# A convolution stem's gradients on one core: the weight gradient's tiles of two batches laid side by side, and the order of all engines planned with other transfer costs

## The chip, the core and the metric

The kernel runs on one core of a Trainium2 chip. The metric is device microseconds of one launch on that core; a figure for a kernel is the median of several runs. A profile is one execution of its own, recorded by the hardware profiler.

The core has engines that run side by side: TensorE (PE; its weight loads are PEld), VectorE (DVE), ScalarE (ACT), GpSimd (POOL) and SyncE (SP), which issues nearly all transfers here. All of them take their instructions in order, each from a queue of its own, and wait for each other by semaphores. A transfer runs on 16 DMA engines after it has been issued.

## What is computed

A strided convolution over time, a normalisation over the whole sequence, GELU, and then all gradients. B = 2 batches, T = 16000 steps, D = 256 channels, K = 31 taps, stride 2, L = 7985 outputs, all in bf16:

```python
h = jnp.einsum('blc,cd->bld', x[:, 0:s * L:s, :], w[0])
for i in range(1, K):
    h = h + jnp.einsum('blc,cd->bld', x[:, i:i + s * L:s, :], w[i])
mu = jnp.einsum('bld->bd', h)[:, None, :] / L
var = jnp.einsum('bld->bd', (h - mu) ** 2)[:, None, :] / L
h = (h - mu) / jnp.sqrt(var + 1e-5)
h = h * gn_gamma[None, None, :] + gn_beta[None, None, :]
return _gelu(h)
```

The outputs are this result and, for a given `grad_out`, the gradients of x, of w (31 x 256 x 256), of gamma and of beta.

## The kernel before, in words

**Stages.** F0 is the forward convolution of batch 0; F1 that of batch 1, with normalisation and GELU of batch 0 beside it; G0 is the gradient of x for batch 0, with GELU of batch 1 beside it; G1 the gradient of x for batch 1; W the gradient of w for both batches. Beside G0 and G1, `dl_turn` turns each piece of the gradient round with DMA transposes (L555) and writes it to DRAM (`dld`) in 128 KB pieces (L550), from where W reads it.

**The arithmetic.** The convolution is split by the bits of the tap number into nested fast convolutions: at each of three levels a pair of taps gives three products, A (the first), C (the second) and B (of the sums), in place of four. In W the two outer levels make nine parts (`COMBOS`, a loop `n` over 0 to 8), the third level is done inside a part. So a part needs sums of x tiles and differences of gradient tiles, made by DVE: `w_add` (L1533) adds two x tiles of 128 x 4096, `pair_x` (L1630) adds neighbouring columns of x tiles, `leaf_d` (L1713) and `pair_d` (L1639) subtract rows of the gradient tiles. The matmuls of W (`w_mm`, L1565) take these sums as they are done; `w_emit` (L1594) adds up finished taps and sends them out.

**Tiles of W.** All of SBUF is one tile, `arena`; the kernel hands out byte ranges of it by hand (`sb(offset, shape)`). For each part and batch there are two x tiles (`x_tile`, loaded by `x_raw`, 1 MB each, in 1 KB runs) and one gradient tile `D2` of 19 rows of 256 columns (`d_tile`): ten even rows and nine odd ones, in two transfers of 640 and 576 KB. Two sets of x tiles, `XS_` and `XT_`, serve even and odd parts; the next part's are loaded while this one computes.

**One instruction for both batches.** `both(u, v, dims)` (L1623) makes an access pattern whose outermost step is the distance from batch 0's view to batch 1's. `pair_x`, `pair_d` and `leaf_d` use it for their inputs and outputs, so that one DVE instruction serves both batches, wherever the two tiles lie. In `XS_` the two first tiles lie at bytes 165376 and 190336, and two tiles of `XT_` at 173696 and 182016, between them; the two others of `XS_` lie at 86016 and 40960, so that the step is negative. In `D2_` the tiles of the batches follow each other, so that the step goes over the rest of batch 0's rows.

**The order.** The kernel body records operations with `plan.add(engine, duration, outputs, inputs, function, ...)`. `Plan.cells` (L266) turns the views into 32-byte cells, and operations that share cells depend on each other: it looks at a pattern's real pieces. `Plan.order` (L317) goes backward and gives each operation a due time from TensorE's own order, less a lead: `self.lead` (L53) holds one number per kind of operation and stage, `self.fine` (L162) a further one per part of a stage. `Plan.listing` (L335) then runs a model of the engines and of the DMA queue, with the costs that each `add` was given, and writes at each moment the ready operation with the earliest due time. `emit` builds the instructions in that order, which is held on every engine. The semaphores and their waits are set by the framework afterwards, from the access patterns.

**Costs of transfers.** `load` (L542) charges SP 0.25 + 0.0005 n us for issuing n packets, `turn` (L552, a DMA transpose) 0.15 + 0.00105 n and at least 1.24.

The lines by which the profile names the work: L550 `load`, L555 `turn`, L744 matmuls of F, L1332 matmuls of G, L839 ACT's copies out of PSUM, L1399 sums on DVE in G, L1214 to L1225 `e_comp` (a gradient tile put together), L1234 its spreading by ACT, L1285 differences in G, L690 sums of weights.

Of the kernel before, what the change touches and what calls it, by code (L numbers as in the profile page):

```python
# [12 lines left out]
ACT = mybir.ActivationFunctionType  # L13
ALU = mybir.AluOpType
# [24 lines left out]
class Plan:  # L39
# [3 lines left out]
    def __init__(self, tc):  # L43
# [10 lines left out]
            "F0 f_evac last": -9.0,  # L54
            "F0 f_mm f_leaf": -119.5,
            "F0 f_mm f_outer": -14.0,
            "F0 f_mm f_three_ac": -8.0,
            "F0 f_mm f_three_b": 32.5,
            "F0 f_mm pe_turn": -75.5,
            "F0 f_outer forward": -106.0,  # L60
            "F0 f_seed forward": -12.0,
            "F0 f_three_b forward": -26.5,
            "F0 keep f_evac": -48.0,
            "F0 load f_evac": 33.0,
            "F0 load put": 9.5,
            "F0 load x_load": 13.5,
            "F0 tt f_sums": -72.0,
            "F0 tt third": 4.5,
            "F0 turn w2_part": -15.5,
            "F0 turn x_load": 24.0,  # L70
            "F0 ve f_first": -78.0,
            "F0 ve_neg f_seed": 20.5,
            "F0 w_sub f_first": 12.0,
            "F0 w_sum w2_part": 26.0,
            "F0 zero f_evac": -11.0,
            "F1 f_evac last": -30.0,
            "F1 f_mm f_leaf": -44.0,
            "F1 f_mm f_outer": -28.0,
            "F1 f_mm f_three_ac": 0.5,
            "F1 f_mm f_three_b": -5.5,  # L80
            "F1 f_outer forward": -3.0,
            "F1 f_seed forward": 11.5,
            "F1 f_three_b forward": 4.0,
            "F1 gelu_unit gelu_batch": -1.0,
            "F1 keep f_evac": 15.5,
            "F1 load gelu_unit": 30.0,
            "F1 tiny elem_finalize": -71.5,
            "F1 tt f_sums": -53.0,
            "F1 tt gelu_unit": -16.5,
            "F1 tt second": -25.5,  # L90
            "F1 tt third": -8.0,
            "F1 turn gelu_unit": -8.0,
            "F1 turn x_load": 45.0,
            "F1 ve f_seed": -22.5,
            "F1 ve_neg f_seed": 5.5,
            "F1 zero f_evac": 10.0,
            "G0 cp e_comp": 11.5,
            "G0 g_mm g_three_b": -9.0,
            "G0 g_three_b input_grad": 6.5,
            "G0 gelu_batch conv_stem_kernel": -7.5,  # L100
            "G0 gelu_unit gelu_batch": -1.0,
            "G0 keep g_evac": -7.0,
            "G0 keep g_seed": 6.0,
            "G0 load dl_turn": 8.0,
            "G0 load e_load": 14.5,
            "G0 load g_evac": -13.5,
            "G0 load gelu_unit": 1.5,
            "G0 load load_w2": 19.5,
            "G0 plus g_seed": 5.0,
            "G0 tiny elem_finalize": -9.0,  # L110
            "G0 tt first": -44.0,
            "G0 tt gelu_unit": -0.5,
            "G0 tt second": 1.0,
            "G0 tt third": -10.5,
            "G0 turn gelu_batch": 4.0,
            "G0 w_sum load_w2": -31.0,
            "G0 zero e_comp": 8.0,
            "G0 zero gelu_batch": -63.0,
            "G1 cp e_comp": -17.5,
            "G1 e_comp e_load": 13.0,  # L120
            "G1 g_mm g_leaf": -6.0,
            "G1 g_mm g_outer": -7.0,
            "G1 g_mm g_three_ac": -8.0,
            "G1 g_mm g_three_b": -5.5,
            "G1 g_three_b input_grad": -238.0,
            "G1 keep g_evac": 3.5,
            "G1 load dl_turn": 11.0,
            "G1 load e_load": -5.5,
# [3 lines left out]
            "G1 spread g_seed": -73.5,  # L132
            "G1 tt first": 3.5,
            "G1 tt second": -15.5,
            "G1 tt third": -43.5,
            "G1 turn dl_turn": 3.5,
            "G1 zero e_comp": 0.5,
            "W keep w_keep": -8.0,
            "W keep weight_grad": 1.0,
            "W leaf_d weight_grad": 6.5,  # L140
            "W load d_tile": -32.5,
            "W load out0_late": 21.0,
# [5 lines left out]
            "W turn out0_late": -36.5,  # L148
            "W ve w_done": 31.5,
# [5 lines left out]
            "W w_emit weight_grad": -64.5,  # L155
            "W w_mm w_leaf": 0.5,
            "W w_pairs weight_grad": -65.0,
# [5 lines left out]
            "F0 f_evac last": {1: 13.5, 2: 6.5, 3: -9.0},  # L163
            "F0 f_mm f_outer": {0: 25.5, 2: -12.0, 3: -48.0},
            "F0 f_mm f_three_ac": {0: -9.5, 1: -3.0, 2: -20.5, 3: -3.0},
            "F0 f_mm f_three_b": {0: 3.0, 2: -87.0, 3: -60.5},
            "F0 f_seed forward": {0: 19.5, 2: 58.0},
            "F0 f_three_b forward": {1: 27.0},
            "F0 keep f_evac": {2: 9.5},
            "F0 load f_evac": {0: 47.5, 3: 4.5},  # L170
            "F0 load put": {0: 20.5, 1: -24.0, 2: 28.0},
# [4 lines left out]
            "F0 turn x_load": {0: -17.0, 2: -24.5},  # L176
            "F0 ve f_first": {0: 33.5},
            "F0 ve f_seed": {0: 30.0, 2: 31.5},
            "F0 ve_neg f_seed": {0: 19.5, 2: -68.5, 3: 41.0},
            "F0 w_sum w2_part": {1: 17.0, 2: -9.5, 3: -32.5},  # L180
            "F0 zero f_evac": {3: 28.0},
            "F0 zero x_load": {3: 58.5},
            "F1 f_evac last": {0: 1.5, 1: 15.0},
            "F1 f_mm f_leaf": {2: -59.5, 3: -91.0},
            "F1 f_mm f_three_ac": {1: -39.0, 2: -69.5, 3: -2.5},
            "F1 f_mm f_three_b": {1: 14.5, 2: 2.0},
            "F1 f_outer forward": {3: 2.0},
            "F1 f_seed forward": {3: 3.0},
            "F1 f_three_b forward": {1: 6.5, 3: -28.5},
            "F1 gelu_unit gelu_batch": {0: -28.0, 1: -2.5, 2: 1.0, 4: 0.5, 6: 6.0, 7: 3.0},  # L190
            "F1 keep f_evac": {3: -7.5},
            "F1 load gelu_unit": {0: -17.0, 2: -9.5, 4: 31.0, 5: -40.5},
            "F1 load out0_store": {7: 37.0},
            "F1 tt f_sums": {0: 2.0},
            "F1 tt gelu_unit": {0: 3.5, 6: -46.0},
            "F1 tt third": {1: 27.5, 3: -11.5},
            "F1 turn gelu_batch": {0: -35.5},
            "F1 turn gelu_unit": {0: 58.0, 6: 25.0},
            "F1 turn x_load": {1: 21.0, 2: 15.0, 3: -71.5},
            "F1 ve f_seed": {3: 24.5},  # L200
            "F1 ve_neg f_seed": {3: 2.0},
            "F1 zero f_evac": {3: 5.5},
            "G0 cp e_comp": {0: -9.5, 2: -7.0},
            "G0 e_comp e_load": {0: -19.0, 1: 5.5, 2: -5.0, 3: 19.5},
            "G0 g_mm g_leaf": {0: -1.5, 3: -25.0},
            "G0 g_mm g_three_ac": {0: 0.5, 1: -1.0, 3: 17.5},
# [264 lines left out]
def conv_stem_kernel(  # L471
# [13 lines left out]
    nc = tc.nc  # L485
# [1035 lines left out]
    for k, o in (("early", 110720), ("late", 57344)):  # L1521
        PD[k] = [(sb(o + 4096 * i, 4, 512), sb(o + 8192 + 4096 * i, 2, 4, D)) for i in range(2)]
# [347 lines left out]
```

## Time and profile before

| | before |
|---|---|
| median of 3 runs | 1212.95 us (1208.56 to 1215.85) |
| the profiled execution | 1214.13 us, of which its span is 1212.4 us |
| TensorE busy | 1138.9 us (94%) |
| DVE busy | 982.9 us (81%) |
| ACT busy | 569.1 us (47%) |
| transfers | 243.55 MB, mean 201 GB/s |
| mean granted TensorE clock | 0.980 |

The span goes from the first to the last instruction of the profiled execution. A busy share says how long an engine had an instruction in it; the rest is time in which it waited, and the profile names what ended each wait. A timeline row has the start, the time, the engine, the line, the operation with its output and input, the count, and in brackets the idle time ahead of it with what ended it. In rows of the chain of waits stand start, length and what the time was spent on; for a DMA that is the time from its issue to its landing. The granted clock is the share of the full TensorE clock that the chip allowed in a stretch. By the program, F0 and F1 end around 435 us, G0 and G1 around 865 us, and W fills the rest.

### The profile page before, as it was taken

The numbers are of one execution on the slowest core, as the hardware profiler recorded it, in microseconds if no ns is written. First come the engines' busy times: TensorE is split into PE (matmuls) and PEld (weight loads), VectorE is DVE, ScalarE is ACT, GpSimd is POOL, SyncE is SP. The second block draws the span as 40 slices with busy tenths as digits, with TensorE's granted clock in tenths as the row PEclk, the third lists the DMA queues.
The fourth block names the chain that finished last, engine by engine and source line by source line (L and its number), as shares of the span: only waits on it lengthen the run. The fifth ranks groups of instructions, "written<-read, shape, count | busy, mean of one in ns | idle before, by whom it ended". The sixth has DMA issues, their size and how long they took to land.

```text
span 1212.4 us, 18743 instructions
## 1 busy us (share of the span) xinstructions
PE 1138.9 (94%) x7645; PEld 757.9 (63%) x7700; DVE 982.9 (81%) x856; ACT 569.1 (47%) x849; POOL 27.2 (2%) x77
## 2 busy tenths in 40 slices
PE   5999999999999999899987999999599999898998
PEld 4888899777778944444443434444278666565685
DVE  7988787798999979796866576875599997677995
ACT  1354445688766687886734556544222212111200
POOL 0000000000000110000000000100000000000000
PEclk8999999999999999999999999999899999998999
DMA  9566945889785979998888566676958825988655
GB/s 208 85 145 137 205 129 142 197 184 211 163 187 146 342 241 242 263 235 234 224 192 217 135 178 180 180 187 168 334 145 254 279 95 175 336 262 287 211 153 149
DMA packets 378061, 243.55 MB, mean 201 GB/s; under 512 B 233377, under 2 KB 353831, under 8 KB 373799
## 3 DMA queue, kind: packets, MB, share of 16 engines
q1 hardware_dynamic: 377783, 242.35, 74.4%
q8 instruction: 60, 0.98, 0.3%
q14 instruction: 26, 0.21, 0.1%
q0 software_dynamic: 192, 0.00, 0.0%
HBM read 106.24 MB, written 80.25 MB: 154 GB/s over the span
## 4 chain that ended last, share of the span: by engine, by line
PE 31%; DMA 8%; DVE 7%; SPq 3%; issue 1%; ACT 1%; DVEq 0%; POOL 0%
PE ps L1565 17%; PE ps L1332 13%; DMA arena<-in_x_dram 3%; DMA arena<-dld 3%; DVE arena L1533 2%; SPq L550 2%; DVE ps L1399 1%; DVE arena L1630 1%; DMA arena<-arena 1%; SPq L555 1%; DVE arena L1639 1%; ACT arena L839 1%; DMA dld<-arena 1%; DMA arena<-hd 1%; DVE arena L1713 1%
## 5 line engine op out<-in xcount | busy, mean ns | idle before, releaser
L1332 PE MATMUL ps<-arena 128*128 128x512 bf16 (+1 forms) x1880 | 416.3, 379 | 28.5 <-DVE ps L1399 7.2
L744 PE MATMUL ps<-arena 128*128 128x256 bf16 (+4 forms) x3460 | 408.4, 282 | 12.9 <-DMA arena<-in_x_dram 5.8
L744 PEld LDWEIGHTS <-arena 128*128 128x128 bf16 x3460 | 339.2, 99 | 82.2 <-DMA arena<-in_x_dram 6.1
L1332 PEld LDWEIGHTS <-arena 128*128 128x128 bf16 x1920 | 189.0, 98 | 254.5 <-issue 39.9
L1565 PE MATMUL ps<-arena 128*128 128x256 bf16 (+1 forms) x2305 | 314.8, 299 | 28.4 <-DVE arena L1630 24.9
L1565 PEld LDWEIGHTS <-arena 128*128 128x128 bf16 x2320 | 229.7, 99 | 113.8 <-DVE arena L1630 27.3
L839 ACT ACTIVATE arena<-ps 128x1024 f32<-128x1024 f32 (+1 forms) x143 | 145.3, 1021 | 291.9 <-PE ps L1565 95.7
L702 DVE TENSOR_TENSOR arena<-arena 128x2080 bf16<-128x2080 bf16 (+7 forms) x126 | 156.2, 1264 | 32.3 <-PE ps L744 26.2
L1399 DVE TENSOR_TENSOR ps<-ps,arena 128x2048 f32<-128x2048 f32 x40 | 91.7, 2294 | 20.4 <-PE ps L1332 12.4
L1285 DVE TENSOR_TENSOR arena<-arena 128x1032 bf16<-128x1032 bf16 (+1 forms) x120 | 84.4, 726 | 28.6 <-PE ps L1332 23.2
L1119 DVE TENSOR_TENSOR arena<-arena 128x2048 bf16<-128x2048 bf16 (+1 forms) x80 | 95.5, 1195 | 14.7 <-ACT arena L1111 7.2
L1533 DVE TENSOR_TENSOR arena<-arena 128x4096 bf16<-128x4096 bf16 x38 | 86.2, 2284 | 19.4 <-DMA arena<-in_x_dram 17.9
L1655 ACT COPY ps<-ps 128x256 f32<-128x256 f32 x54 | 19.3, 357 | 93.3 <-PE ps L1565 92.2
L859 ACT ACTIVATE arena<-ps 128x512 bf16<-128x512 f32 (+1 forms) x64 | 37.1, 580 | 52.9 <-PE ps L744 50.3
L1639 DVE TENSOR_TENSOR arena<-arena 128x2048 bf16<-128x2048 bf16 x38 | 46.3, 1221 | 13.5 <-DMA arena<-dld 9.0
L1630 DVE TENSOR_TENSOR arena<-arena 128x4096 bf16<-128x4096 bf16 x19 | 43.3, 2284 | 10.8 <-DMA arena<-in_x_dram 10.4
L1399 DVE TENSOR_TENSOR arena<-ps,arena 128x2048 f32<-128x2048 f32 x16 | 36.6, 2289 | 18.0 <-ACT arena L839 14.6
L1109 DVE SCALAR_TENSOR_TENSOR arena<-arena 128x2048 bf16<-128x2048 bf16 (+1 forms) x16 | 35.8, 2236 | 17.0 <-ACT arena L1106 16.5
L780 ACT ACTIVATE ps<-ps 128x256 f32<-128x256 f32 x75 | 27.8, 371 | 40.0 <-PE ps L744 38.7
L1713 DVE TENSOR_TENSOR arena<-arena 128x4608 bf16<-128x4608 bf16 x18 | 45.6, 2550 | 0.1
L1234 ACT COPY arena<-arena 128x768 bf16<-128x768 bf16 (+1 forms) x64 | 36.5, 616 | 19.2 <-DVE arena L1225 15.8
L814 ACT ACTIVATE arena<-ps 128x512 f32<-128x512 f32 x56 | 29.5, 601 | 25.1 <-PE ps L744 19.7
(78 smaller groups left out, 637.9 us busy)
## 6 DMA issues: line engine op xcount, KB each, us to landing
arena<-in_x_dram SPq DMA_DIRECT2D x40, 1024.0 KB
dld<-arena SPq DMA_DIRECT2D x144, 128.0 KB
arena<-hd SPq DMA_DIRECT2D x32, 512.0 KB
out_dram<-arena SPq DMA_DIRECT2D x14, 1024.0 KB
arena<-dld SPq DMA_DIRECT2D x18, 640.0 KB
arena<-dld SPq DMA_DIRECT2D x18, 576.0 KB
vl<-arena SPq DMA_DIRECT2D x36, 256.0 KB
arena<-vl SPq DMA_DIRECT2D x9, 1024.0 KB
```

What stands on the lines that cost most here:

```text
L702: lambda: nc.vector.tensor_tensor(out=o, in0=a, in1=b, op=ALU.add))
L744: yield nc.tensor.matmul(ps[:, dh, cs], lhsT=wt, rhs=mv, start=s0, stop=False, skip_group_check=True)
L839: lambda: nc.scalar.activation(out=out, in_=ps, func=ACT.Copy, scale=scale))
L1119: add("DVE", dve(nf), [o], [a, b_], lambda: V.tensor_tensor(out=o, in0=a, in1=b_, op=op))
L1285: lambda: nc.vector.tensor_tensor(out=o, in0=a, in1=b, op=ALU.subtract))
L1332: yield nc.tensor.matmul(ps[:, e, 0:wide], lhsT=lt, rhs=mv, start=s0, stop=False, skip_group_check=True)
L1399: lambda: nc.vector.tensor_tensor(out=o, in0=a, in1=b, op=ALU.add))
L1533: add("DVE", dve(4096), [o], [a, b], lambda: nc.vector.tensor_tensor(out=o, in0=a, in1=b, op=ALU.add))
L1565: yield nc.tensor.matmul(ps[:, s, c0:c1], lhsT=lt, rhs=mv, start=s0, stop=False, skip_group_check=True)
L1630: add("DVE", dve(4096), [o], i, lambda: nc.vector.tensor_tensor(out=o.rearrange("p b (f c) -> p b f c", c=512), in0=i[0], in1=i[1], op=ALU ...
L1639: add("DVE", dve(2048), [o], [u, v], lambda o=o, u=u, v=v: nc.vector.tensor_tensor(out=o, in0=u, in1=v, op=ALU.subtract))
L1713: add("DVE", dve(4608), [o], [u, v], lambda: nc.vector.tensor_tensor(out=o, in0=u, in1=v, op=ALU.subtract))
```

## The change

Four things are changed.

1. The gradient tiles of W are laid out anew: the even rows of both batches next to each other (`D2E_`), then the odd rows of both (`D2O_`). The outputs of `pair_d` are interleaved in the same way (`PD`): both batches of one half, then both of the other.
2. `pair_x` takes one instruction for both batches only where the second x tile lies at most 4352 elements behind the first; otherwise it takes two, one per batch. That is so for the five `pair_x` that read `XS_` directly. W has then 179 DVE operations in place of 174.
3. `load` and `turn` charge SP other costs.
4. The two tables of leads are replaced throughout, for all five stages.

The diff, with the tables cut to their first lines:

```diff
@@ Plan.__init__
         self.lead = {
-            "F0 f_evac last": -9.0,
-            "F0 f_mm f_leaf": -119.5,
-            "F0 f_mm f_outer": -14.0,
+            "F0 f_evac last": -14.5,
+            "F0 f_mm f_leaf": -67.5,
+            "F0 f_mm f_outer": 14.0,
...
         self.fine = {
-            "F0 f_evac last": {1: 13.5, 2: 6.5, 3: -9.0},
+            "F0 f_evac last": {0: 17.5, 3: -12.5},
...
@@ load, turn
-        add(eng, {"POOL": 0.74, "SP": 0.25 + 0.0005 * np_, "ACT": 0.4}[eng], [out], [in_],
+        add(eng, {"POOL": 0.74, "SP": 0.42 + 0.00016 * np_, "ACT": 0.4}[eng], [out], [in_],
...
-        add("SP", max(1.24, 0.15 + 0.00105 * np_), [out], [in_],
+        add("SP", max(1.3, 0.15 + 0.00125 * np_), [out], [in_],
...
@@ tiles of W
-    D2_ = [[sb(o + 9728 * i, 19, D) for i in range(2)] for o in (0, 127424)]
+    D2E_ = [[sb(o + 5120 * i, 10, D) for i in range(2)] for o in (0, 127424)]
+    D2O_ = [[sb(o + 10240 + 4608 * i, 9, D) for i in range(2)] for o in (0, 127424)]
...
-    PD = {"all": [(sb(16384 + 4096 * i, 4, 512), sb(o, 2, 4, D)) for i, o in enumerate((73728, 77824))]}
-    for k, o in (("early", 110720), ("late", 57344)):
-        PD[k] = [(sb(o + 4096 * i, 4, 512), sb(o + 8192 + 4096 * i, 2, 4, D)) for i in range(2)]
+    PD = {k: [(sb(o + 4096 * i, 4, 512), sb(u, 2, 2, 4, D)[:, :, i]) for i in range(2)]
+          for k, o, u in (("all", 16384, 73728), ("early", 110720, 118912), ("late", 57344, 65536))}
@@ d_tile
-        for j, (r, k) in enumerate(((0, 10), (10, 9))):
+        for j, (v, k) in enumerate(((D2E_[n > 0][b], 10), (D2O_[n > 0][b], 9))):
             t = dl_d[b][3 * i1 + i2][j]
-            load(D2_[n > 0][b][:, r:r + k].rearrange("p r d -> p (r d)"),
+            load(v.rearrange("p r d -> p (r d)"),
@@ pair_x
-        o = both(p[0][0], p[1][0], [[1, 2048]])
-        i = [both(x[0][:, j], x[1][:, j], [[1024, 4], [1, 512]]) for j in range(2)]
-        add("DVE", dve(4096), [o], i, lambda: nc.vector.tensor_tensor(out=o.rearrange("p b (f c) -> p b f c", c=512),
-                                                                      in0=i[0], in1=i[1], op=ALU.add))
+        if 0 <= x[1].offset - x[0].offset <= 4352:
+            o = both(p[0][0], p[1][0], [[1, 2048]])
+            i = [both(x[0][:, j], x[1][:, j], [[1024, 4], [1, 512]]) for j in range(2)]
+            add("DVE", dve(4096), [o], i, lambda: nc.vector.tensor_tensor(out=o.rearrange("p b (f c) -> p b f c", c=512),
+                                                                          in0=i[0], in1=i[1], op=ALU.add))
+            return
+        for (o, _), v in zip(p, (x[0], x[1])):
+            add("DVE", dve(2048), [o], [v], lambda o=o, v=v: nc.vector.tensor_tensor(
+                out=o, in0=v[:, 0:8:2], in1=v[:, 1:8:2], op=ALU.add))
@@ weight_grad
-            D2, XSUM = D2_[n > 0], XSUM_[n > 0]
+            D2, DO, XSUM = D2E_[n > 0], D2O_[n > 0], XSUM_[n > 0]
...
-                u, v = (both(D2[0][:, k], D2[1][:, k], [[D, 9], [1, D]]) for k in (o_, 10))
+                u, v = (both(t[0][:, k], t[1][:, k], [[D, 9], [1, D]]) for t, k in ((D2, o_), (DO, 0)))
...
-                w_pairs(X[h], h, pm, D2, 11, 2)
-            pair_d(pm, D2, 12, 10, 11)
+                w_pairs(X[h], h, pm, DO, 1, 2)
+            pair_d(pm, DO, 2, 0, 1)
```

More of the change, by code (lines that the diff above doesn't have):

```diff
@@ L81, in __init__ @@
[L81 to L93, printed above, removed]
@@ new lines, in __init__ @@
+            "F0 load f_evac": 62.5,
+            "F0 load put": 10.5,
+            "F0 tt f_sums": -97.0,
+            "F0 tt second": 16.5,
+            "F0 ve_neg f_seed": -25.0,
+            "F0 w_sub f_first": 8.0,
+            "F0 w_sum w2_part": 5.0,
+            "F0 zero x_load": 16.5,
+            "F1 f_evac last": -54.0,
+            "F1 f_mm f_leaf": -235.5,
+            "F1 f_mm f_three_ac": -3.5,
+            "F1 f_mm f_three_b": -20.5,
+            "F1 f_outer forward": 3.5,
+            "F1 f_seed forward": 3.0,
@@ L162, in __init__ @@
         self.fine = {
-            "F0 f_evac last": {1: 13.5, 2: 6.5, 3: -9.0},
[L164 to L171, printed above, removed]
[4 rows of a table removed]
@@ L186, in __init__ @@
[L186 to L195, printed above, removed]
```

291 lines of the change are left out of this document (159 added, 132 removed), and 4 rows, old and new, of the table MIR.

## The prediction

> **What bounds the kernel now.** I read the page first, then busy time by stretch, then who waited for whom on TensorE, then the timelines of the engines around each long gap of TensorE.
>
> ```profile
> span 1212.4 us, 18743 instructions
> ...
> PE 1138.9 (94%) x7645; PEld 757.9 (63%) x7700; DVE 982.9 (81%) x856; ACT 569.1 (47%) x849; POOL 27.2 (2%) x77
> ```
>
> TensorE is busy for 1138.9 of 1212.4 us. The change leaves its 7,700 matmuls as they are, so it can win only what lies between them: 73.5 us, and the time that a halved clock adds to busy time. The table by stretch says where that is (length, then busy time and count of PE, PEld, DVE, ACT, POOL, then granted clock, DMA share, GB/s):
>
> ```profile
> 23.00:435.00 412.00, 411.06 (x3450) 338.47 (x3453) 359.17 (x359) 245.21 (x450) 8.87 (x19) 0.99 0.73 179
> 435.00:634.00 199.00, 186.31 (x848) 84.88 (x863) 164.72 (x177) 148.69 (x172) 9.40 (x23) 0.99 0.88 225
> 634.00:665.00 31.00, 22.54 (x99) 10.03 (x100) 20.67 (x23) 12.17 (x18) 0.58 (x3) 0.94 0.83 216
> 665.00:865.50 200.50, 193.31 (x876) 87.64 (x892) 139.00 (x108) 104.22 (x116) 5.47 (x17) 0.99 0.69 182
> 865.50:881.30 15.80, 0.02 (x1) 0.02 (x2) 6.86 (x4) 1.02 (x1) 0.00 (x0) 0.57 1.10 358
> 881.30:884.80 3.50, 3.50 (x17) 2.52 (x18) 3.50 (x2) 0.00 (x0) 0.00 (x0) 0.51 0.38 86
> ...
> 1056.60:1059.80 3.20, 0.03 (x2) 0.01 (x1) 3.20 (x3) 1.02 (x1) 0.00 (x0) 0.84 1.10 350
> 1059.80:1065.60 5.80, 5.80 (x28) 4.12 (x29) 5.80 (x3) 1.07 (x3) 0.00 (x0) 0.50 1.10 349
> ...
> 1100.90:1106.40 5.50, 0.01 (x2) 0.01 (x1) 5.50 (x4) 1.02 (x1) 0.00 (x0) 0.71 0.84 266
> 1106.40:1110.00 3.60, 3.60 (x18) 2.56 (x19) 3.60 (x3) 1.02 (x1) 0.00 (x0) 0.50 0.89 251
> ```
>
> The forward pass after 23 us has 0.9 us of idle TensorE in 412: nothing to win. The middle (435 to 865.5) idles 12.7 + 8.5 + 7.2 = 28.4 us in many pieces. The weight gradient starts at 865.5 with a hole of 15.8 us and has two more of 3.2 and 5.5 us; behind each of the three TensorE runs at half clock for 3.4, 5.8 and 3.6 us, half of which is lost (1.7, 2.9, 1.8). In all three holes the engine that comes last is DVE with a sum at L1630, `pair_x`.
>
> **The change part by part: the hole at the start of W.** DVE's timeline there, SP's issues, the chain of waits, and the sizes of the transfers:
>
> ```profile
> 861.72 2.28 DVE L1533 TENSOR_TENSOR arena<-arena 128x4096 bf16<-128x4096 bf16 x1
> 874.41 2.29 DVE L1630 TENSOR_TENSOR arena<-arena 128x4096 bf16<-128x4096 bf16 x1 [10.41 <-DMA arena<-in_x_dram]
> ```
> ```profile
> 855.32 1.41 SPq L550 DMA_DIRECT2D arena<-dld  x1
> 858.80 0.55 SPq L550 DMA_DIRECT2D arena<-in_x_dram  x1
> 859.39 2.22 SPq L550 DMA_DIRECT2D arena<-dld  x3
> ```
> ```profile
> 862.15 12.14 DMA arena<-in_x_dram
> ```
> ```profile
> arena<-in_x_dram SPq DMA_DIRECT2D x40, 1024.0 KB
> ...
> arena<-dld SPq DMA_DIRECT2D x18, 640.0 KB
> arena<-dld SPq DMA_DIRECT2D x18, 576.0 KB
> ```
>
> The `pair_x` at 874.41 waits 10.41 us for the transfer issued at 862.15, which lands at 862.15 + 12.14 = 874.29. By the addresses it needs nothing of it: the sum reads the tiles at bytes 165376 and 190336 with one pattern, and the transfer writes the next part's tile at 173696, which lies between them. The build puts a wait on everything that a pattern spans. The change gives this sum its own two instructions, and in the order of the built program with its waits each of the two waits for its own tile alone. Over the whole stage, DVE's waits for a transfer on which no address depends fall from 16 to 2.
>
> What is late next is the last tile that the first matmuls truly need: the transfer issued at 858.80, then a `w_add` (2.28 us) and the other `pair_x` (2.29). I put its landing back from 874.29 by what was issued after it, three `arena<-dld` of 640, 576 and 576 KB and the 1,024 KB of 862.15: 2,816 KB or 2.88 MB, at the 358 GB/s of the stretch 865.5 to 881.3, is 8.1 us, so 866.2. The new order issues both 576 KB halves ahead of it where one 640 KB half was: 512 KB or 1.5 us more, 867.7. The two sums take 4.6, so TensorE starts at 872.3 in place of 881.3: **9.0 us** won. Ends: a load takes from 6.1 us (a row below) to 12.14, so it lands between 864.9 and 870.9, which gives 11.8 to 5.8. The remaining hole of 7 us still ends in a cold start, so the 1.7 us stay lost.
>
> **The holes at 1056 and 1101.** DVE again, and the chain ahead of the second:
>
> ```profile
> 1050.34 4.62 DVE L1533 TENSOR_TENSOR arena<-arena 128x4096 bf16<-128x4096 bf16 x2 [3.69 <-DMA arena<-in_x_dram]
> 1056.31 1.22 DVE L1639 TENSOR_TENSOR arena<-arena 128x2048 bf16<-128x2048 bf16 x1 [1.36 <-DMA arena<-dld]
> 1057.46 2.28 DVE L1630 TENSOR_TENSOR arena<-arena 128x4096 bf16<-128x4096 bf16 x1
> ```
> ```profile
> 1092.14 1.21 DVE L1639 TENSOR_TENSOR arena<-arena 128x2048 bf16<-128x2048 bf16 x1
> 1099.58 1.23 DVE L1639 TENSOR_TENSOR arena<-arena 128x2048 bf16<-128x2048 bf16 x1 [6.23 <-DMA arena<-dld]
> 1100.72 2.28 DVE L1533 TENSOR_TENSOR arena<-arena 128x4096 bf16<-128x4096 bf16 x1
> 1102.92 1.22 DVE L1594 TENSOR_TENSOR arena<-ps,arena 128x1024 bf16<-128x1024 f32 x1
> 1104.06 2.28 DVE L1630 TENSOR_TENSOR arena<-arena 128x4096 bf16<-128x4096 bf16 x1
> ```
> ```profile
> 1079.56 9.21 DMA arena<-in_x_dram
> ...
> 1093.38 6.11 DMA arena<-dld
> ```
>
> At 1056 a `pair_d` (L1639) stands ahead of the `pair_x` and waits for a half of the gradient tile that its pattern spans and does not read. Afterwards only the odd halves are spanned, they are issued first, and in the built order the `pair_x` stands right behind the `w_add`s, which end at 1050.34 + 4.62 = 1054.96: `pair_x` ends at 1057.2, TensorE starts at 1057.3 in place of 1059.8. **2.5 us**, and with a hole of only 0.7 us the clock stays up: **2.9 us** more.
>
> At 1093 the wait is a loop: the transfer of 1093.38 was held back until the `pair_d` of 1092.14 had read, by a span again, and the next `pair_d` then waited 6.23 us for that transfer. Both go. DVE's work behind the last true landing (1079.56 + 9.21 = 1088.77) is in the new order two `w_add`s, a half `pair_x`, the `pair_x` and two `w_emit`s: 2.3 + 2.3 + 1.2 + 2.3 + 2.4 = 10.5, to 1099.3, ahead of the 1100.9 at which TensorE runs out. **5.5 us** and the 1.8 of the cold start. Each of these two terms is nothing at worst, if the tile itself comes later by that much.
>
> **The clock.** For the hole of 3.17 us the price of 2.9 rests on rows; another hole of about that length cost none:
>
> ```profile
> 654.86:657.87 3.01, 0.00 (x1) 0.00 (x0) 2.98 (x4) 0.00 (x0) 0.00 (x0) 1.00 1.05 339
> 657.87:663.00 5.13, 5.08 (x25) 2.54 (x26) 5.13 (x5) 1.02 (x1) 0.00 (x0) 1.00 0.13 18
> ```
>
> So a remainder of some 3 us may or may not keep the loss. The Trainium skill, TensorE: Matmul & The Clock Gate, section on HAM oscillation, asks for no TensorE gaps above about 3.4 us; by it the hole of 3.2 us should have been free, and the row at clock 0.50 behind it says otherwise. By that rule the sum would be better by 2.9 us only if a hole of 3 us remained at 1056; with 0.7 us both give the same.
>
> **The splits.**
>
> ```profile
> L1639 DVE TENSOR_TENSOR arena<-arena 128x2048 bf16<-128x2048 bf16 x38 | 46.3, 1221 | 13.5 <-DMA arena<-dld 9.0 <-PE ps L1565 3.7
> L1630 DVE TENSOR_TENSOR arena<-arena 128x4096 bf16<-128x4096 bf16 x19 | 43.3, 2284 | 10.8 <-DMA arena<-in_x_dram 10.4 <-PE ps L1565 0.2
> ```
>
> Five `pair_x` become two halves each: 2 x 1221 - 2284 = 158 ns, 0.8 us over the stage, hidden beside TensorE except the one at the start, where it is in the wait for the tile. The new strides of the gradient tiles cost nothing that a row shows: sizes and inner runs are the same.
>
> **The order with the measured issue cost.** The planner charged a 128 KB `dld<-arena` 0.25 + 0.0005 x 256 = 0.378 us of SP; it will charge 0.42 + 0.00016 x 256 = 0.461. The rows of SP's issues from 586 to 850, then TensorE, ACT and DVE in that stretch:
>
> ```profile
> L550 SPq DMA_DIRECT2D dld<-arena x100: 367/488/2031, 585.8 to 845.1; - x100
> ```
> ```profile
> 639.46 15.40 PE L1332 MATMUL ps<-arena 128*128 128x512 bf16 x63 [5.34 <-ACT ps L839]
> 657.87 2.32 PE L1332 MATMUL ps<-arena 128*128 128x256 bf16 x11 [3.01 <-DVE ps L1399]
> ```
> ```profile
> 637.66 0.83 ACT L1234 COPY arena<-arena 128x768 bf16<-128x768 bf16 x1 [5.94 <-DVE arena L1225]
> ```
> ```profile
> 630.66 0.81 DVE L1214 TENSOR_SCALAR arena<-arena,stats 128x2048 bf16<-128x2048 bf16 x1 [5.82 <-DMA arena<-hd]
> ```
>
> 100 of these at 0.488 - 0.378 = 0.11 us make 11 us by which SP falls behind the plan in the input gradient. The rows show the effect: DVE waits 5.82 us for an `arena<-hd`, the copy at L1234 behind it on ACT waits 5.94, and ACT's copy out of PSUM that TensorE needs stands in order behind that. The stalls of 5.34 and 3.01 us are 8.4 together. Planned with the true cost, the same transfers are to stand earlier. But all stages are reordered (of SP's 711 issues some 170 leave their place relative to the rest, of DVE's 824 some 190), and the trace cannot show what new stalls come. Upper end: all 28.4 us of the middle; lower end: as many stalls of this kind again, 8 us lost. I take **6 us** won, near the two stalls. The forward pass is reordered too; at 0.9 us of idle it can only lose, 0 to 4; I take 0, since DVE there is busy 359 of 412 and has a tenth to spare.
>
> **The sum**, from the profiled execution's 1214.1 (span 1212.4 and 1.7 around it; 1.2 above the median of the three runs): 9.0 + 2.5 + 2.9 + 5.5 + 1.8 + 6 = 27.7; 1214.1 - 27.7 = 1186.4, say **1187**.
>
> **Rivals.**
>
> *The transfers bound W anyway.* From 1056.6 to 1065.6 the DMA share is 1.10, the highest of the table, and parts that fetch eight 1 MB tiles need them within some 40 us. Then the holes at 1056 and 1101 only change their name, the reorder gives nothing, and 9 us are won: 1205. Against it: at 1065.6 to 1100.9 the share falls to 0.84 while DVE waits on its loop. Its price is a delay of the last tile by 2.5 to 5.5 us at each hole.
>
> *Slower: ACT's in-order queue in the input gradient.* If the new order again puts L1234's copies ahead of the copies out of PSUM while their tile is late, each chunk costs a stall like the 5.34 us one. W wins 21.7 (9.0 + 5.4 + 7.3); it is used up by four such stalls, and with six it is 1214.1 - 21.7 + 32 = 1224. It decides from the fifth chunk on. For it: the chain above exists. Against: it did so at one of the chunks now.
>
> *The patterns still span others.* Then only the reorder is left: 1214.1 - 6 = 1208. The waits in the built order speak against it.
>
> **How the numbers follow.** My forecast and what lies near it (1172 to 1200): 0.79. Transfers bound W: 0.11 (1200 to 1207). Patterns still span: 0.03. Slower by ACT's queue or by another stall of the reorder: 0.07, of which 0.04 by over 0.5%. About 0.5%, 6 us, is what a measurement of this kernel tells from no change. Faster: 0.79 + 0.08 of the rivals = 0.87; within: 0.09; slower: 0.04. Range: the terms' lower ends (11.8, 5.4, 7.3 and 17 of the middle) give 1172; the upper side takes in the transfer rival, 1205.
>
> **What would show it.** In the profile after: the first L1565 matmul of W behind a hole of 5 to 9 us, with an L1630-like half sum no longer waiting for a transfer issued after its own; no hole above 2 us with clock 0.50 in the later parts; DVE's waits `<-DMA arena<-dld` near zero at `pair_d`; idle TensorE between 435 and 865 down from 28 to about 22. I am wrong if `w_add` (L1533) takes over the waits for `in_x_dram` by as much as L1630 and L1639 lose, or if the middle shows more and longer stalls behind ACT.

## The result, and the profile after

| | before | after |
|---|---|---|
| median of four runs (lowest to highest) | 1213.37 us (1208.56 to 1215.85) | 1193.49 us (1190.87 to 1197.82) |
| ratio, 95% interval | | 0.9844 [0.9802, 0.9887] |
| profiled execution / its span | 1214.13 / 1212.4 | 1190.87 / 1189.1 |
| TensorE's last matmul of the input gradient ends | 865.47 | 865.56 |
| hole at the start of W | 15.81 | 5.46 |
| TensorE idle, 435 us to that point | 28.3 | 26.5 |
| TensorE idle in W behind the first hole | 12.6 | 4.4 |

The changed kernel takes 1.56% [1.13, 1.98] less, by this ratio 18.9 us (the medians lie 19.9 apart). (The idle times and the ends are summed from the matmuls' rows of each trace.) The line numbers are some six higher: `w_add` is L1539, `pair_x` L1637 and in halves L1641, `pair_d` L1650, W's matmuls L1571. First the page after, then busy time by stretch (length; PE, PEld, DVE, ACT, POOL; granted clock, DMA share, GB/s), cut at the same stages as the table of before:

```profile
span 1189.1 us, 18747 instructions
...
PE 1136.3 (96%) x7645; PEld 756.0 (64%) x7700; DVE 981.3 (83%) x861; ACT 568.9 (48%) x849; POOL 26.2 (2%) x77
```
```profile
435.00:634.00 199.00, 185.69 (x838) 84.08 (x853) 162.28 (x174) 149.08 (x172) 7.22 (x23) 0.98 0.89 221
634.00:665.00 31.00, 25.04 (x108) 10.95 (x108) 18.36 (x21) 10.81 (x16) 0.58 (x3) 0.94 0.94 238
665.00:865.50 200.50, 193.27 (x874) 87.64 (x892) 145.36 (x114) 105.33 (x118) 6.58 (x17) 0.99 0.72 190
865.50:871.10 5.60, 0.14 (x2) 0.09 (x2) 4.72 (x3) 1.02 (x1) 0.00 (x0) 0.98 1.06 362
871.10:1050.00 178.90, 176.03 (x1340) 132.50 (x1349) 157.09 (x93) 38.59 (x60) 0.00 (x0) 0.99 0.72 226
1050.00:1100.00 50.00, 48.67 (x316) 31.10 (x319) 43.69 (x29) 7.02 (x13) 0.00 (x0) 1.00 0.93 307
1100.00:1185.00 85.00, 84.79 (x652) 63.91 (x653) 73.46 (x53) 8.38 (x16) 0.53 (x1) 1.00 0.65 195
```

Read the first three rows against those of before: 185.69 for 186.31, 25.04 for 22.54, 193.27 for 193.31. TensorE idles 1.8 us less in the middle but is busy 1.8 us longer (404.0 for 402.2): it ran there for 13.7 us at half clock, before for 10.2. So the middle ends 0.1 us later than before, and the whole gain lies in W. There the hole of 15.8 us is 5.5 (the row's 5.60 is the length of the cut), and the stretch 1050 to 1185, which held the holes of 3.2 and 5.5 us and the half clock behind them, runs at clock 1.00. DVE's timeline shows how W starts now:

```profile
856.79 1.22 DVE L1641 TENSOR_TENSOR arena<-arena 128x2048 bf16<-128x2048 bf16 x1
...
862.32 1.22 DVE L1641 TENSOR_TENSOR arena<-arena 128x2048 bf16<-128x2048 bf16 x1
866.35 2.29 DVE L1539 TENSOR_TENSOR arena<-arena 128x4096 bf16<-128x4096 bf16 x1 [2.81 <-DMA arena<-in_x_dram]
868.67 2.29 DVE L1637 TENSOR_TENSOR arena<-arena 128x4096 bf16<-128x4096 bf16 x1
```

The two half sums run without a wait, and the last wait is `w_add`'s for the tile it reads. Over the whole kernel DVE's groups of these lines say the same (last column: idle time ahead of the group and what ended it):

```profile
L1539 DVE TENSOR_TENSOR arena<-arena 128x4096 bf16<-128x4096 bf16 x38 | 86.1, 2286 | 21.0 <-DMA arena<-in_x_dram 20.1 <-PE ps L1571 0.7
...
L1650 DVE TENSOR_TENSOR arena<-arena 128x2048 bf16<-128x2048 bf16 x38 | 45.4, 1218 | 1.8 <-PE ps L1571 1.8
...
L1637 DVE TENSOR_TENSOR arena<-arena 128x4096 bf16<-128x4096 bf16 x14 | 31.9, 2286 | 0.2
```

`pair_d` waited 9.0 us for `arena<-dld` and now waits for none; `pair_x` waited 10.4 us for `arena<-in_x_dram` and now 0.2 in all. In the middle the stalls did not go, they moved. TensorE's timeline after:

```profile
571.91 20.12 PE L1338 MATMUL ps<-arena 128*128 128x512 bf16 x79 [4.51 <-ACT ps L1365]
...
641.56 2.65 PE L1338 MATMUL ps<-arena 128*128 128x512 bf16 x7 [3.72 <-ACT arena L845]
```

Before, the long ones there were 5.34 at 634 and 3.01 at 655.

### The profile page after: what moved, and what is told of

Same layout as the page of the kernel before. It is cut to its first block, busy times and chain, and to the rows that moved or that the text cites. A ratio compares the mean times of both kernels' runs of the same rounds, so it can differ in the third digit from the quotient of the medians.

```text
span 1189.1 us, 18747 instructions
## 1 busy us (share of the span) xinstructions
PE 1136.3 (96%) x7645; PEld 756.0 (64%) x7700; DVE 981.3 (83%) x861; ACT 568.9 (48%) x849; POOL 26.2 (2%) x77
## 2 busy tenths in 40 slices
DMA packets 378061, 243.55 MB, mean 205 GB/s; under 512 B 233377, under 2 KB 353831, under 8 KB 373799
## 4 chain that ended last, share of the span: by engine, by line
PE 55%; DVE 14%; DMA 11%; SPq 9%; ACT 7%; issue 3%; DVEq 0%; ACTq 0%; another core or an unknown queue 0%
PE ps L750 21%; PE ps L1571 19%; PE ps L1338 16%; SPq L561 5%; SPq L556 4%; DMA arena<-in_x_dram 3%; DMA arena<-dld 2%; DVE arena L1125 2%; DVE arena L708 2%; DVE ps L1405 2%; DMA arena<-dyd 1%; DMA yd<-arena 1%; ACT arena L845 1%; DVE arena L1539 1%; ACT arena L1117 1%
## 5 line engine op out<-in xcount | busy, mean ns | idle before, releaser
L1338 PE MATMUL ps<-arena 128*128 128x512 bf16 (+1 forms) x1880 | 418.4, 380 | 26.7 <-ACT ps L1365 10.3
L1338 PEld LDWEIGHTS <-arena 128*128 128x128 bf16 x1920 | 189.2, 99 | 254.6 <-issue 39.9
L1571 PE MATMUL ps<-arena 128*128 128x256 bf16 (+1 forms) x2305 | 309.7, 296 | 9.9 <-DVE arena L1637 6.2
L1571 PEld LDWEIGHTS <-arena 128*128 128x128 bf16 x2320 | 227.6, 98 | 92.1 <-DVE arena L1637 7.0
L708 DVE TENSOR_TENSOR arena<-arena 128x2064 bf16<-128x2064 bf16 (+7 forms) x126 | 156.3, 1266 | 32.7 <-PE ps L750 31.2
L1539 DVE TENSOR_TENSOR arena<-arena 128x4096 bf16<-128x4096 bf16 x38 | 86.1, 2286 | 21.0 <-DMA arena<-in_x_dram 20.1
L1405 DVE TENSOR_TENSOR arena<-ps,arena 128x2048 f32<-128x2048 f32 x16 | 36.6, 2288 | 16.2 <-ACT arena L845 12.8
L1724 DVE TENSOR_TENSOR arena<-arena 128x4608 bf16<-128x4608 bf16 x18 | 45.6, 2551 | 3.7 <-DMA arena<-dld 3.7
L1115 DVE SCALAR_TENSOR_TENSOR arena<-arena 128x2048 bf16<-128x2048 bf16 (+1 forms) x16 | 35.8, 2237 | 13.7 <-ACT arena L1112 13.7
L1650 DVE TENSOR_TENSOR arena<-arena 128x2048 bf16<-128x2048 bf16 x38 | 45.4, 1218 | 1.8 <-PE ps L1571 1.8
L1110 ACT ACTIVATE arena<-arena,stats 128x1024 bf16<-128x1024 bf16 (+1 forms) x32 | 37.7, 1210 | 11.5 <-DMA yd<-arena 8.6
L1240 ACT COPY arena<-arena 128x768 bf16<-128x768 bf16 (+1 forms) x64 | 36.5, 616 | 13.5 <-DVE arena L1231 12.8
```

Of the source, the lines that this page charges most:

```text
L708: lambda: nc.vector.tensor_tensor(out=o, in0=a, in1=b, op=ALU.add))
L1338: yield nc.tensor.matmul(ps[:, e, 0:wide], lhsT=lt, rhs=mv, start=s0, stop=False, skip_group_check=True)
L1405: lambda: nc.vector.tensor_tensor(out=o, in0=a, in1=b, op=ALU.add))
L1539: add("DVE", dve(4096), [o], [a, b], lambda: nc.vector.tensor_tensor(out=o, in0=a, in1=b, op=ALU.add))
L1571: yield nc.tensor.matmul(ps[:, s, c0:c1], lhsT=lt, rhs=mv, start=s0, stop=False, skip_group_check=True)
L1724: add("DVE", dve(4608), [o], [u, v], lambda: nc.vector.tensor_tensor(out=o, in0=u, in1=v, op=ALU.subtract))
```

## Experiments

Theory 1, from the forecast: the gain comes from waits that patterns put on tiles they do not read. Theory 2: it comes from the new order. The change makes both at once, and a planner lays the order anew for any edit, so the order was pinned: the planner's order of the 3,202 operations of one kernel was written down as a list, which the other kernel then emits.

```
-        for i in self.order():
+        for i in EMIT:          # the operations' numbers in a fixed order
```

**e1_waits_only: new layout and splits, old order.** Edit: the changed kernel with the list of the kernel before.

> The changed kernel's layout and its five split pair_x, with every operation of every engine kept in the order of the kernel before (no new costs, no new tables; the two halves of a split sum stand where the fused one stood). Theory 1, the gain in W comes from the patterns that no longer span other tiles: up to 865.5 us the trace is that of before, W starts behind a hole of about 7 us in place of 15.8, and the holes at 1056 and 1101 shrink to under 2; W takes 325 to 335 us in place of 346.9, the whole 1192 to 1202. Theory 2, the gain comes from the new order: W keeps its three holes, 1210 to 1215. In between: the hole at the start goes, the two later ones stay because in the old order a pair_d with its true wait still stands ahead of the pair_x, 1203 to 1207.

Measured 1190.49 us (1189.67 to 1195.62), ratio 0.9825 [0.980, 0.985]. Its table by stretch: the input gradient, the hole, W.

```profile
435.00:866.40 431.40, 404.21 (x1826) 183.19 (x1861) 326.67 (x308) 266.52 (x306) 15.19 (x43) 0.99 0.79 205
866.40:872.60 6.20, 0.05 (x2) 0.01 (x1) 5.47 (x4) 1.02 (x1) 0.00 (x0) 0.73 1.04 392
872.60:1184.30 311.70, 309.26 (x2305) 227.72 (x2320) 274.61 (x173) 53.81 (x88) 0.53 (x1) 0.99 0.75 235
```

The removed waits alone give 1.75% [1.5, 2.0], 21.2 us: no less than the whole change. The two intervals overlap, so which of the two kernels is faster is not told apart. The time lies 1.5 us below the expected range. Theory 1 holds.

**e2_order_only: new order, old layout and fused sums.** Edit: the kernel before with the list of the changed kernel.

> The kernel before, its layout and its fused pair_x kept, with every operation in the order of the changed kernel (a fused sum stands where the later of its halves stands). Theory 1: the first pair_x of W waits again for the transfer issued behind its own, the hole at the start of W is 12 to 16 us in place of 5.5, and two or more holes of over 2 us come back behind pair_d and pair_x later; 1205 to 1216. Theory 2: W keeps its short holes, 1189 to 1195. For the middle both expect the stalls of the changed kernel (4.5 us at 567, 3.7 at 638), since no pattern that changed is read there.

Measured 1211.17 us (1207.53 to 1216.75, ten runs), ratio 0.9976 [0.9955, 0.9997]. The hole and W:

```profile
862.60:878.80 16.20, 0.02 (x1) 0.00 (x0) 6.84 (x4) 1.02 (x1) 0.00 (x0) 0.63 0.92 354
878.80:1205.80 327.00, 314.69 (x2305) 229.84 (x2320) 275.81 (x169) 53.97 (x88) 0.53 (x1) 0.98 0.69 213
```

All of W's holes are back (16.2, then 12.3 us idle in all). The order alone is worth 0.24% [0.03, 0.45], 2.9 us [0.4, 5.5], in the old layout. On top of the new layout nothing of it is seen: the changed kernel's median is 1193.49, that of e1 with the old order 1190.49. Theory 2 falls.

**e3_split_only and e4_layout_only: the two halves of the change to W, old order.** e3 is the kernel before with the split of `pair_x` alone, e4 the kernel before with the new places of the gradient tiles alone (what reads them follows):

```
e3
+        if 0 <= x[1].offset - x[0].offset <= 4352:
...
+        for (o, _), v in zip(p, (x[0], x[1])):
+            add("DVE", dve(2048), [o], [v], ...
e4
-    D2_ = [[sb(o + 9728 * i, 19, D) for i in range(2)] for o in (0, 127424)]
+    D2E_ = [[sb(o + 5120 * i, 10, D) for i in range(2)] for o in (0, 127424)]
+    D2O_ = [[sb(o + 10240 + 4608 * i, 9, D) for i in range(2)] for o in (0, 127424)]
...
+    PD = {k: [(sb(o + 4096 * i, 4, 512), sb(u, 2, 2, 4, D)[:, :, i]) for i in range(2)]
```

> The kernel before in its own order, with the five pair_x that span a foreign tile split into two halves, and the gradient tiles laid out as before. Theory 1: the hole at the start of W falls from 15.8 to about 7 us, the holes at 1056 (3.2) and 1101 (5.5) stay, since the wait there is that of a pair_d on the gradient tiles: 1203 to 1207. Rival: the hole stays at 15 us, since the transfer that the first sum truly needs lands just as late: 1211 to 1215.

> The gradient tiles and their difference tiles laid out as in the changed kernel, the five pair_x left fused, every operation in the order of the kernel before. Theory 1, each false wait has its own price: W still starts behind a hole of about 16 us, and the holes at 1056 (3.2) and 1101 (5.5) shrink to under 2 with no half clock behind them: the forecast's 5.4 + 7.3 = 12.7 less, 1199 to 1203. Rival, the parts overlap (the later holes only stayed away in the run with both because W started earlier): 1206 to 1214.

Measured: e3 1203.54 us (1202.29 to 1206.81), 0.9928 [0.9903, 0.9952]; e4 1201.82 us (1201.24 to 1203.52), 0.9899 [0.987, 0.9927]. The hole and W of e3, then of e4:

```profile
868.50:874.10 5.60, 0.01 (x1) 0.00 (x0) 5.43 (x4) 1.02 (x1) 0.00 (x0) 0.73 1.03 395
874.10:1198.60 324.50, 312.23 (x2305) 228.24 (x2320) 276.46 (x173) 53.88 (x88) 0.53 (x1) 0.99 0.73 226
```
```profile
867.40:883.40 16.00, 0.00 (x0) 0.00 (x0) 6.80 (x4) 1.02 (x1) 0.00 (x0) 0.59 1.11 347
883.40:1195.90 312.50, 309.63 (x2305) 227.49 (x2320) 274.44 (x169) 53.79 (x88) 0.53 (x1) 0.99 0.72 225
```

Each part takes away its own holes and leaves the other's: e3 has the short start (5.6) and the long W (324.5), e4 the long start (16.0) and the short W (312.5). 0.72% and 1.01% add to 1.73%; e1 measured 1.75% for both.

**e7_costs_only: the new issue costs alone, planned anew.** Edit to the kernel before:

```
-        add(eng, {"POOL": 0.74, "SP": 0.25 + 0.0005 * np_, ...
+        add(eng, {"POOL": 0.74, "SP": 0.42 + 0.00016 * np_, ...
-        add("SP", max(1.24, 0.15 + 0.00105 * np_), ...
+        add("SP", max(1.3, 0.15 + 0.00125 * np_), ...
```

> The kernel before with the new issue costs of SP alone (0.42 + 0.00016 per packet, 1.3 us per transpose); its layout, its fused sums and its tables of leads stay, so that the planner lays the order anew by the costs alone. The forecast's step, that an order planned with the true cost wins 6 us of the middle: 1206 to 1210, with the gain between 435 and 866. Rival, the order cannot win where SP's queue is full: 1211 to 1217. On the other side, the leads are tuned to the old costs and no longer fit: over 1217.

Measured 1248.02 us (1246.67 to 1251.96), ratio 1.0282 [1.0242, 1.0322]: the other side. The forward pass, the input gradient, and W behind its hole:

```profile
23.00:435.00 412.00, 402.59 (x3391) 333.84 (x3394) 353.78 (x344) 236.03 (x434) 7.48 (x19) 0.98 0.70 174
435.00:886.30 451.30, 416.75 (x1880) 188.95 (x1915) 329.93 (x322) 274.77 (x321) 20.05 (x43) 0.98 0.77 200
...
901.60:1242.90 341.30, 317.50 (x2305) 230.55 (x2320) 276.38 (x169) 54.00 (x88) 0.53 (x1) 0.97 0.66 206
```

Every stage loses: TensorE idles for 9.4 us in the first row (0.9 before), and the two others are 20.8 and 13.8 us longer than before. Costs nearer to the measured ones, in a planner whose leads were set with the old ones, made the order worse by 34 us. With the new tables as well, the new order ends near where the old one was, so the tables must have made that up; they were not run with the old costs.

**e5_queue_moves: does ACT's queue hold the middle?** The changed kernel's list with sixteen operations moved by hand: ACT's `gelu_unit` steps behind the `g_three_b` copy and `keep g_seed` at 567, the `spread` copies of L1240 (with the two zeroings that wait for them) behind three copies at 638, a half `pair_x` behind a `plus g_seed` at 858, three transfers behind the last x tile at 853.

> The changed kernel with four places of its order changed by hand. On ACT, the copies that TensorE needs stand ahead of work whose tile comes late: the copy for g_three_b ahead of two gelu steps (stall of 4.51 us at 567.4), three copies out of PSUM and to SBUF ahead of four spread copies of e_comp (3.72 us at 637.8). On DVE, a half pair_x stands behind the plus that TensorE waits for (2.30 us at 858.0). On SP, the two 1 MB and 576 KB loads at the start of W change places so that the last x tile is issued ahead of a gradient half (5.46 us at 865.6). Theory, the missing 6 us of the middle went into in-order queues: the first two gaps fall under 1 us, the third to about 1.2, the fourth to about 3.7; 4 + 3.3 + 1.1 + 1.7 = 10 us, and with the half clock behind the first three gone (half of 6.8 + 3.4 + 3.4) about 17: 1173 to 1183. Rival: the stalls wait for the same late transfers at the next instruction of the queue, and the time stays at 1189 to 1196.

Measured 1195.68 us (1190.36 to 1202.93), 0.9863 [0.9821, 0.9904]: nothing won. The profiled execution is the slowest of the four; its middle is idle for 28.8 us. TensorE, then DVE and ACT ahead of its last stall (L1476 is L1338 here, L1503 is L1365, L1378 is L1240):

```profile
585.42 1.02 PE L1476 MATMUL ps<-arena 128*128 128x512 bf16 x4 [2.64 <-ACT arena L983]
...
592.32 26.50 PE L1476 MATMUL ps<-arena 128*128 128x256 bf16 x121 [1.89 <-DVE ps L1543]
...
655.64 4.59 PE L1476 MATMUL ps<-arena 128*128 128x512 bf16 x11 [6.70 <-ACT ps L1503]
```
```profile
650.43 0.75 DVE L1360 TENSOR_SCALAR arena<-arena,stats 128x2048 bf16<-128x2048 bf16 x1 [4.86 <-DMA arena<-dyd]
```
```profile
653.54 1.56 ACT L1378 COPY arena<-arena 128x768 bf16<-128x768 bf16 x2 [6.13 <-DVE arena L1369]
655.01 0.58 ACT L1503 COPY ps<-ps 128x512 f32<-128x512 f32 x1
```

The stalls at 567 and 638 are gone as meant. In place of 4.51 us there are 2.64 + 1.89 = 4.53 some 15 to 23 us later, in place of 3.72 there are 6.70 at 649, behind the next chunk's `arena<-dyd`. The copy order decided where TensorE stood, not how long: the rival holds. In these rows two spread copies (L1378) again stand ahead of the copy out of PSUM (L1503), so the edit moved the place at which ACT's queue holds TensorE and left the next one; an order without any such place was not run. What is late behind it is the transfer, and the question is whether its issue or its bytes make it late. SP issued for 131.7 us of the 140 from 500 to 640 before and 126.4 after, summed from its rows: its queue is full.

**e6_pool_queue and e8_half_stores: SP's queue or the bytes?** Both are e1 with one edit. e6 lets GpSimd issue the 144 stores of 128 KB (L550 sends everything over 4 KB to SP):

```
-        if plan.stage in ONE and nbytes > 4096:
+        if plan.stage in ONE and nbytes > 4096 and sys._getframe(1).f_code.co_name != "dl_turn":
             eng = "SP"
```

e8 emits nothing for the second store of each pair, and `d_tile` loads the first's rows twice.

> The layout and splits of the changed kernel in the order of the kernel before (1190.5 measured), and the 144 stores of 128 KB of the gradient leaves issued by GpSimd's queue in place of SP's. Theory A, SP's issuing sets the pace of the input gradient (it issues for 17 to 19 of every 20 us from 500 to 640): about 0.49 us x 100 of SP's time fall away between 586 and 845, and the long stalls between 435 and 866 (2.5 + 4.1 + 3.0 + 2.1 and their half clock) shrink by half or more, 1180 to 1187. Theory B, the transfers themselves are late (the DMA share is 0.8 to 1.1 there): 1188 to 1194. On the other side, if GpSimd's own issue is dearer than SP's, or its zeroing and copying waits behind the stores, over 1196.

> The layout and splits of the changed kernel in the order of the kernel before, with the second of the two stores of each gradient leaf left out: 72 stores of 128 KB less of SP's issuing, some 35 us of it, and 9.4 MB less to move; the weight gradient then reads the first store's rows in place of the second's, in loads of the same size, so that out_2 is not the reference's. Theory A (SP's issuing) and theory B (the transfers) both expect the stalls between 435 and 866 to shrink by half or more: 1178 to 1186; together with the run in which GpSimd issues the stores this tells A from B. Theory C, neither: the stalls come from the order of the engines' own work, and they stay: 1188 to 1193.

Measured: e6 1176.87 us (1175.7 to 1179.38), 0.9694 [0.9664, 0.9723]; e8 1169.83 us (1168.99 to 1172.79), 0.9637 [0.9608, 0.9666]. The input gradient of e6 and of e8, then the stores in e1 and in e6 (ns: least, median, most; in the other row busy us and mean ns):

```profile
435.00:850.80 415.80, 398.52 (x1818) 181.74 (x1853) 326.25 (x308) 264.60 (x305) 120.20 (x189) 1.00 0.81 211
```
```profile
435.00:848.80 413.80, 400.50 (x1837) 183.09 (x1872) 327.05 (x309) 268.65 (x309) 15.51 (x43) 1.00 0.75 194
```
```profile
L694 SPq DMA_DIRECT2D dld<-arena x144: 362/494/2032, 451.4 to 855.5; - x144
```
```profile
L694 POOL DMA_DIRECT2D dld<-arena x144 | 104.1, 725 | 281.0 <-DMA arena<-arena 268.8 <-issue 10.8 <-DMA dld<-arena 1.4
```

With the same bytes moved (211 GB/s for e1's 205) the input gradient takes 415.8 us in place of 431.4, and the middle idles 17.3 us in place of 27.2. e8, where half the stores and their bytes are gone and the other half stays on SP, ends the input gradient 2 us earlier still. So e6's gain needs no byte less, only a shorter SP queue, though a store costs GpSimd 725 ns and SP 494: GpSimd had the time. GpSimd's stores go as fewer and larger packets (345,806 in all for 378,061), but the DMA engines' busy time is the same, 907 us for e1's 908 as a mean of the 16. Both times lie below their expected ranges, e6 by 3 us and e8 by 8. Theory A holds for e6. Whether it is the issue time itself or the number of transfers that one queue holds open, e6 does not tell apart; and since SP still issues for 122 of the 140 us from 500 to 640 in e8, against 108 in e6, what the missing bytes add in e8 stays open. The Trainium skill, DMA: Bandwidth & Descriptors, section Issuing engines are not separate DMA queues, says that issuing from several engines saves only sequencer time, and calls that usually small beside the DMA itself. Here a store's issue is short as well (0.49 us on SP), but the 144 moved stores were worth 13.6 us together, by the medians of e1 and e6.

**e11_pool_alone, e9_pool_new_order, e10_first_sum_split: what adds to what.** e11 makes e6's edit in the kernel before, old order and layout. e9 is e6 with the changed kernel's order. e10 is e6 with the first `pair_x` split too and one gradient half of 640 KB issued behind the last x tile.

> The kernel before, its layout, its fused sums and its order, with the 144 stores issued by GpSimd's queue. If SP's full queue and the false waits are two causes that don't touch, the 13 to 14 us of the queue come off here too and the three holes of W stay: 1198 to 1202. Rival, relieving SP also brings W's tiles in time, so that part of the false waits is hidden: 1188 to 1196. On the other side, the false waits take back what the input gradient wins, since W's transfers go no faster: 1205 to 1212.

> The changed kernel, its own order, with the 144 stores of 128 KB of the gradient leaves issued by GpSimd's queue in place of SP's. Theory A: with SP's queue relieved the new order has nothing left to hide, so it is worth what it was with the full queue, 0 to 3 us beside the old order (1176.9 measured): 1173 to 1180, idle TensorE from 435 to the end of the input gradient 15 to 19 us. Rival: the new order was laid for SP's costs and its gain shows only where SP isn't full: 1165 to 1171. On the other side, the order puts GpSimd's zeroing and copying behind stores that wait: over 1184.

> The old order with the changed layout and GpSimd's stores (1176.9 measured), with two edits at the start of W: the first pair_x is split too, its first half ahead of the second w_add, and the gradient half of 640 KB that only leaf_d reads is issued behind the last x tile and not ahead of it. Theory, the hole is the landing of the last x tile plus the two sums behind it: 1.1 us less of DVE and about 1.7 us (640 KB at 358 GB/s) less of landing, the hole falls from 6.7 to about 4 us; the time 1173 to 1177. Rival, the first matmuls then wait for a gradient half in place of the x tile: hole 5.5 to 7, time 1175 to 1179.

Measured: e11 1200.24 us (1194.75 to 1206.16), 0.9875 [0.9826, 0.9924]; e9 1182.39 us (1177.27 to 1186.13), 0.9724 [0.9679, 0.977]; e10 1176.09 us (1173.93 to 1178.23), 0.9669 [0.9634, 0.9705]. The hole of e11, then TensorE's wait at the start of W in e10:

```profile
847.70:863.70 16.00, 0.05 (x2) 0.01 (x1) 6.85 (x4) 1.02 (x1) 0.00 (x0) 0.63 1.11 352
```
```profile
PE ps L1709 <- DMA arena<-dld: 5.9, 1, 5.9
```

e11: SP's relief and the false waits are separate causes, 1.25% and 1.75% beside 3.06% for both (e6). e9: the new order is not better with a relieved queue either; its median is 5.5 us above e6's, the intervals overlap, and the time lies between the ranges that were expected. e10: the hole only fell from 6.7 to 5.9 us, since the first matmuls then wait for a gradient half, as its rival said; the time is e6's and fits both expectations. e6 and e10 are faster than both kernels: by over 3% than before, and by some 1.4% than after by the medians.

## Why the prediction was right, and where it was wrong

The forecast was 1187, the result 1193.5: inside the range, 6.5 us above. In the profiled executions W gave 23.7 us where 21.7 were forecast, and the middle -0.1 where 6 were: one term failed. (The profiled execution after is the fastest of its four, 2.6 us below their median.)

- *Hole at the start of W, 9.0 us.* Right. The hole fell by 10.4 in the trace of after, and the split alone gave 0.72% [0.48, 0.97], 8.7 us. The mechanism is the one named: the half sums no longer wait, and the last x tile then ends the hole. Its `w_add` started at 866.35, where the forecast had put the landing at 867.7. The cold start stayed: the clock was halved from 870.9 to 874.3.
- *Holes at 1056 and 1101 with their half clock, 5.4 + 7.3 = 12.7.* Right. The layout alone gave 1.01% [0.73, 1.3], 12.3 us. No hole behind 871.1 is over 1.1 us.
- *The price of the first two together, 21.7:* e1 measured 21.2 [18.2, 24.3].
- *The order, 6 us of the middle.* This is the step that failed. The middle's idle time fell from 28.3 to 26.5 us, not to 22, and the order alone is worth 2.9 us [0.4, 5.5] in the old layout, nothing that is seen in the new. The observation was right, that SP is late in the input gradient; the conclusion was not. A new order leaves a queue that issues for 94% of the time nearly as full (90% after): it mainly chooses which transfer is late. I had set the term by the two stalls that would go and gave the ones that come only to the lower bound. Relieving the queue (e6) gave more than twice the 6 us. The range's lower end took 17 us of the middle, a figure that no row gives; no run with SP's queue as it was won as much there.
- *Splits and forward pass at 0.* Nothing in W or before 435 us (0.9 us idle before, 0.6 after) speaks against it.
- *Rival, transfers bound W.* Not so at 1056 and 1101. At the start of W it is so from 6 us down: e10 took the sums out of the way and met a gradient tile.
- *Rival, ACT's in-order queue.* Its mechanism came, twice (4.51 and 3.72 us), about as much as the stalls that went. So it cost the expected gain, not more. By e5's rows and e6's gain, ACT is where the delay is passed on, not where it is made.
- *Rival, patterns still span.* Excluded by DVE's group rows.

What `w_add` took over, from its row before (the one after stands above):

```profile
L1533 DVE TENSOR_TENSOR arena<-arena 128x4096 bf16<-128x4096 bf16 x38 | 86.2, 2284 | 19.4 <-DMA arena<-in_x_dram 17.9 <-PE ps L1565 1.3
```

Its waits for `in_x_dram` were 17.9 us and are 20.1, so it took 2.2 of the 19.4 us (9.0 and 10.4) that the two sums lost; `leaf_d` (L1724) took 3.7 for `arena<-dld`.

## What to carry to other kernels

Where an engine waits for a transfer, look at whether it reads what that transfer writes: in this kernel's build an access pattern that strides over a foreign tile waits for it, and in an in-order queue everything behind it waits too (21 us in e1). Before reordering around late transfers, add up how long the issuing engine issues in that stretch. Here it was nine tenths; the new order alone won 2.9 us, and moving issues to an idle engine 13.6. Pin the order when a planner would otherwise answer an edit with another schedule.

## What the runs showed that was not expected

The clock. The forecast could not say why a hole of 3.17 us was followed by half clock and one of 3.01 was not. In each profile the halved stretches begin and end on a grid of 3.413 us, and what tells the two cases apart is TensorE's busy share of one grid cell. Four pairs of cells of the kernel before (a cell, then the next; busy time first, clock third from the end):

```profile
505.85:509.26 3.41, 1.40 (x7) 0.53 (x6) 3.41 (x6) 3.41 (x6) 0.00 (x0) 1.00 1.17 316
509.26:512.67 3.41, 3.09 (x14) 1.47 (x15) 0.75 (x1) 3.41 (x6) 0.35 (x3) 1.00 1.09 266
553.63:557.05 3.42, 1.40 (x6) 0.58 (x6) 3.04 (x2) 3.16 (x5) 0.00 (x0) 1.00 1.10 309
557.05:560.46 3.41, 3.19 (x10) 1.36 (x9) 3.41 (x4) 3.37 (x2) 0.00 (x0) 0.50 0.97 275
```
```profile
656.03:659.45 3.42, 1.53 (x8) 0.85 (x9) 3.42 (x3) 0.00 (x0) 0.00 (x0) 1.00 0.78 196
659.45:662.86 3.41, 3.41 (x19) 1.62 (x18) 3.41 (x4) 1.02 (x1) 0.00 (x0) 1.00 0.00 0
1055.39:1058.80 3.41, 1.23 (x6) 0.38 (x4) 2.49 (x2) 1.02 (x1) 0.00 (x0) 1.00 1.09 354
1058.80:1062.22 3.42, 2.42 (x12) 1.74 (x13) 3.42 (x3) 0.00 (x0) 0.00 (x0) 0.50 1.10 349
```

Both holes are shared by two cells: the one of 3.17 us puts 2.2 us into its worse cell and leaves it 36% busy, the one of 3.01 us puts 1.8 us there and leaves 45%. Over the 13 profiles, of some 4,300 cells behind the first 45 us, each of the 54 at full clock that were followed by half clock was at most 40.9% busy, and each that was not had at least 41.1%. So, by estimate (59% of 3.413), a gap of some 2.0 us is enough if it falls into one cell, and one of 3 us may pass. A single hole's clock price is then in part luck: the stall of 2.46 us at 575.6 of e1 was followed by a halved cell. This was observed, not set by an experiment. The Trainium skill, TensorE: Matmul & The Clock Gate, Part 1, states the free-running window of 3413 ns, with which the grid agrees. The same page of the Trainium skill, section Why this matters for your kernels, warns of idle gaps over some 3 us between matmul bursts; that rule doesn't carry the share that the rows show, and e1's stall of 2.46 us lies below it.

The prediction's 1.8 and 2.9 us for the two cold starts were rightly read from the rows. Had the grid lain otherwise against the holes, they would by this have been other sizes; that was not run.
